# Spreading the next batch's transform steps over the chunks by their VectorE work instead of evenly

## The chip, the cores and the metric

The kernel runs on one core of one Trainium2 chip. TensorE (PE, with its weight loads shown as PEld) multiplies matrices, VectorE (DVE), ScalarE (ACT) and GpSimd (POOL) work element by element, and SyncE (SP), ScalarE and GpSimd have queues on which transfers are issued. The metric is the device time of one execution in microseconds (us): the median of the runs.

## The reference

For 8 batches of 3008 tokens with 256 features, the reference filters along the tokens in the frequency domain and then applies a two-layer network with a gated activation:

```python
X = np.fft.rfft(x, axis=1)                      # x: (8, 3008, 256)
Y = X * (filt_r + 1j * filt_i)[None]
y = np.fft.irfft(Y, n=3008, axis=1).astype(np.float32)
x = y.reshape(8 * 3008, 256)
h = x @ w_in                                    # w_in: (256, 2048)
g = h * (1.0 / (1.0 + np.exp(-1.702 * h)))
return (g @ w_out).astype(np.float32)           # w_out: (2048, 256)
```

## The kernel before

**The network.** The 3008 tokens of a batch are cut into 6 tiles of up to 512 tokens, and the hidden layer of a tile into 16 chunks of 128 features. One pass of the main loop (`for n, (i, fc) in enumerate(turns)`) is one chunk. `first(fc)` of `mlp` multiplies `w_in` with the tile's `y` in six matmuls of 512 columns (L588), because `y` and the weights are held as a high and a low part. ScalarE applies the activation twice, into `gh` (L591) and back into `h` (L592), and VectorE makes the low part `gl = h - gh` (L593). `second(fc)` multiplies `w_out` with `gh` (four matmuls) and `gl` (two), L603. `ahead` issues `first` of the next chunk before `second` of this one. In tile 5 of every even batch (0, 2, 4, 6) the matmuls are 384 columns wide. The first two tiles of batch 0 alternate in the list `turns`, while the generator `conv` still converts weights (up to chunk 23).

**The transform.** The filter of batch b + 1 is made by the generator `fft(b + 1)` while the chunks of batch b run. Each `yield` ends a step, and there are 46 of them:

- 12 steps of stage 1, two for each of the six loads `x_b_c`. ScalarE makes `xh` (L441), GpSimd `xl` (L442), TensorE runs three matmuls (L274 to L276, `s1`), ScalarE copies the sum into `ah` (L446), and VectorE makes `al` (L447). After both halves of a load, four stores on ScalarE's queue put `ah` and `al` into `a_d` in HBM (L452).
- Two empty steps (`for i in range(2): yield`). In front of them `load` brings `a_d` back as `zy` on GpSimd's queue (L461), and `load_f` the filter into `f_buf` on SP's queue.
- 16 steps `forward(i)`: matmuls `s2` (L475 and L476 for i = 0, L478 otherwise), `halves` (L428 on ScalarE, L429 on VectorE) into `c_buf`, the products with the filter into `u_buf` and `c_buf` (L419 to L421 on VectorE), their sum on GpSimd (L422), two casts into `zy` on VectorE (L492) and two subtractions on GpSimd (L493). Each asks for the loads of i + 2.
- 16 steps `backward(i)`, each one behind its forward: matmuls `i2`, `halves` into `b`, and in every second step two stores to `b_d` in HBM on ScalarE's queue (L508).

**The signal.** `signal(b, t, y)` makes the input `y` of tile t: it loads `br` from `b_d` (SP's queue), multiplies (`i1`, L561 and L563), and copies the high part on ScalarE (L569) and the low part on VectorE (L570). In batch 0 `br` comes by transposes `bt` (L543, L547) from SBUF instead.

**What sets the order.** The steps are called in the main loop:

```python
if n % (6 * NFC) == 0:
    lead = 16 if b == 0 else 0
    done, chunk, chunks = 0, 0, 6 * NFC - lead - 8
...
    while chunk <= chunks and done < STEPS * chunk // chunks:
        run(nxt, 1)
        done += 1
```

with `STEPS = 48`, so one step is called about every 1.5 chunks in batch 0 (72 chunks after a lead of 16) and every 1.83 later (88 chunks). The order of the calls is not the final one. A scheduler places the instructions on each engine, in the order of the calls where it can and earlier where it holds an engine for free. It does so as the program is built, by a model of durations; each engine then runs its list strictly in order. Pools limit it too: `ps_f` has four PSUM buffers, and seven `raw` buffers hold `x`, `ah`, `al`, `b` and `br`.

Of the kernel before, what the change touches and what calls it, by code (L numbers as in the profile page):

```python
# [20 lines left out]
P = 128  # L21
Q = 112
NFC = DFF // P
STEPS = 48

LEAST = 2.0**-15
MOST = float(np.uint32(0x47EFFFFF).view(np.float32))
# [125 lines left out]
def tile_kernel(  # L153
# [56 lines left out]
    def load_unit(i):  # L210

        src = (w_out if i % 2 else w_in)[i // 2]
        if i < EARLY:
            w = early[:, i]
            w = w[:, :, :D] if src.dtype == F32 else w.bitcast(I64)
        elif src.dtype == F32:
            w = raw(f"w_{i}").rearrange("p a d -> p (a d)")[:, 0:512].rearrange("p (a d) -> p a d", a=2)
        else:
            w = sb.tile([P, 2, D], I64, tag="raw", name=f"w_{i}", bufs=7)
        load_in(w, src)  # L220
        units[i] = w
# [47 lines left out]
    b_of, stores, done_w = {}, [], [0]  # L269
# [29 lines left out]
    def split_de():  # L299

        pin = tc.keep_in_program_order
        de_f = table["de"].rearrange("p (m c) -> p m c", m=4)
        pin(nc.scalar.copy(t1_sb[:, 0], table["t1"]))
        pin(nc.vector.tensor_tensor(t1_sb[:, 1], table["t1"], t1_sb[:, 0].bitcast(F32), ALU.subtract))
        pin(nc.gpsimd.memset(de_sb.bitcast(F32), 0.0))
        for k in range(2):
            h, o = slice(64 * k, 64 * k + 48), slice(64 - 64 * k, 112 - 64 * k)
            pin(nc.scalar.copy(de_sb[h, k, :, h], de_f[h, :, h]))  # L310
            pin(nc.vector.tensor_tensor(de_sb[h, k, :, o], de_f[h, :, h], de_sb[h, k, :, h].bitcast(F32), ALU.subtract))
            pin(nc.gpsimd.tensor_copy(de_sb[o, k], de_sb[h, k].bitcast(F32)))
# [118 lines left out]
    def fft(b):  # L431
# [22 lines left out]
                    )  # L454

        b_d = dram.tile([48, 64, D], F32, tag="b_d", name=f"b_d{b}")

        def load(i):
            for k in range(2):
                src = a_d[k].rearrange("n (k s) d -> n k s d", k=2)[:, :, 2 * i : 2 * i + 2, :]  # L460
                nc.gpsimd.dma_start(  # L461
                    zy[0][64 * k : 64 * k + 48, i % 2].rearrange("p k s d -> p k (s d)"),
                    src.rearrange("n k s d -> n k (s d)"),
                )
# [51 lines left out]
        for i in range(17):  # L516
# [3 lines left out]
            if i:  # L520
                backward(i - 1)
                yield
        b_of[b] = b_d

    def signal(b, t, y):

# [91 lines left out]
    def store():  # L618

        while stores:  # L620
            nc.sync.dma_start(*stores.pop(0))

    def run(gen, n=None):
        while n is None or n > 0:
            if next(gen, run) is run:
                return False
            n = None if n is None else n - 1
        return True
# [6 lines left out]
    def start(b, t):  # L635
        ys[b, t] = sb.tile([P, 2, 2, 512], F32R, tag="y", name=f"y_{b}_{t}")
        return signal(b, t, ys[b, t])
# [16 lines left out]
    def ahead(i, fc):  # L654
        if i not in chunks_of:
            b, t = tiles[i]
            chunks_of[i] = mlp(b, t, ys.pop((b, t)), 4 if t < 5 or b % 2 else 3, (ps_f, "f") if i == 1 else (ps_o, "o"))
        chunks_of[i][0](fc)

    ahead(*turns[0])  # L660
    for n, (i, fc) in enumerate(turns):
        b, t = tiles[i]
        if n % (6 * NFC) == 0:

            lead = 16 if b == 0 else 0
            done, chunk, chunks = 0, 0, 6 * NFC - lead - 8
            nxt = fft(b + 1) if b + 1 < B else iter(())
        if n == 0:
            run(start(*tiles[1]))
        if n + 1 < len(turns):  # L670
            ahead(*turns[n + 1])
        chunks_of[i][1](fc)
        if fc == 1:
            store()
        if n < 24:
            run(conv, 1)
            if n % 2 and n < 10:
                load_unit(11 + n // 2)
        if n == 9:
            split_de()  # L680
            in_order[0] = False
        if n == 24:
            zy.append(const.tile([P, 4, 2, 2, D], F32R, tag="zy", name="zy"))
            nc.gpsimd.memset(zy[0][32:64].bitcast(F32), 0.0)
        if b or n >= lead:
            chunk += 1
            while chunk <= chunks and done < STEPS * chunk // chunks:
                run(nxt, 1)
                done += 1
        at = () if i == 0 else (10, 11, 13) if i == 1 else (9, 12, 13) if t == 5 else (1, 3, 9)  # L690
        if fc in at and i + 1 < len(tiles):
            if i + 1 not in sigs:
                sigs[i + 1] = start(*tiles[i + 1])
            run(sigs[i + 1], 1)
            if fc == at[-1]:
                run(sigs[i + 1])
# [29 lines left out]
```

## Time and profile before

| | |
|---|---|
| median of 3 runs | 2399.27 us (2398.87 to 2399.83) |
| profiled execution | 2397.69 us, of which its span is 2395.9 us |
| TensorE busy | 2379.6 us (99%) |
| VectorE busy | 1399.9 us (58%) |
| ScalarE busy | 1302.9 us (54%) |
| GpSimd busy | 722.1 us (30%) |
| chain that ended last | TensorE 94% of the span, VectorE 3% |
| loads of `zy` from `a_d`, issue to landing | 3.6 us, 192 KB each |
| stores of `al` to `a_d`, issue to landing | 3.8 us, 256 KB each |

Matmuls are pipelined, so a matmul's recorded span overlaps the next one's: the distance from one start to the next is what it costs. In a row of the timeline stand the start, the duration, engine, line, operation, what is written and read, the shape, the count, and in brackets the idle time before it with what ended that. A wait for several things is put down to the last.

### The profile page before, as it was taken

The page shows a single profiled execution, that of the slowest core. Times are in us where ns is not written, and L with a number is a line of the kernel's source. Part 1 is how long each engine was busy: PE and PEld are TensorE (multiplying, and loading weights), DVE is VectorE, ACT ScalarE, POOL GpSimd, SP SyncE. Part 2 cuts the span into 40 slices and gives each one's busy share as a digit, 9 for nine tenths or more (in the row PEclk, how much of TensorE's full clock was granted, in tenths as well). Part 3 has the DMA queues.
Part 4 walks back from the last instruction along what each step waited for, and adds up shares of the span by engine and source line. Part 5 has one row for each costly group of instructions (what it writes and reads, how often), then busy time and mean ns, then how long its engine had stood idle before and what let it go on. Part 6 is the DMA issues. An engine that isn't in the chain of part 4 may idle for free.

```text
span 2395.9 us, 31327 instructions
## 1 busy us (share of the span) xinstructions
PE 2379.6 (99%) x11102; PEld 1981.7 (83%) x11102; DVE 1399.9 (58%) x2198; ACT 1302.9 (54%) x2426; POOL 722.1 (30%) x675
## 2 busy tenths in 40 slices
PE   9999999999999999999999999999999999999999
PEld 7887888888888889888888888988888888898887
DVE  8967863886357743667436674467734677322222
ACT  6665655655556555555555555555555555444443
POOL 3025532553234422344213442244422344000000
PEclk9999999999999999999999999999999999999999
DMA  9345444643544435443353433534335342300000
GB/s 346 100 137 113 117 128 130 139 119 89 156 95 106 112 102 140 95 101 95 105 136 93 104 97 102 152 92 106 88 104 143 89 106 75 78 7 9 18 9 18
DMA packets 141484, 248.67 MB, mean 104 GB/s; under 512 B 15376, under 2 KB 81040, under 8 KB 141328
## 3 DMA queue, kind: packets, MB, share of 16 engines
q1 hardware_dynamic: 63088, 136.18, 19.6%
q10 hardware_dynamic: 53152, 66.44, 10.3%
q0 software_dynamic: 25088, 44.05, 9.6%
q8 instruction: 88, 1.44, 0.3%
q14 instruction: 68, 0.56, 0.1%
HBM read 152.76 MB, written 93.85 MB: 103 GB/s over the span
## 4 chain that ended last, share of the span: by engine, by line
PE 94%; DVE 3%; DMA 1%; ACT 1%; issue 1%; POOL 0%; SPq 0%; ACTq 0%; POOLq 0%
PE o L603 41%; PE h L588 41%; PE i L561 3%; PE i L478 2%; PE s L478 2%; PE s L274 1%; PE s L276 1%; PE s L275 1%; DVE gl L593 1%; DVE c_buf L429 0%; PE i L391 0%; DVE u_buf L419 0%; DVE u_buf L420 0%; DMA br<-b_d 0%; PE s L381 0%
## 5 line engine op out<-in xcount | busy, mean ns | idle before, releaser
L588 PE MATMUL h<-y,wi 128*128 128x512 f32 (+1 forms) x4608 | 1151.7, 385 | 0.0
L593 DVE TENSOR_TENSOR gl<-h,gh 128x512 fp32r<-128x512 f32 (+1 forms) x768 | 522.3, 680 | 888.3 <-ACT h L592 877.0
L588 PEld LDWEIGHTS h<-y,wi 128*128 128x128 f32 x4608 | 860.6, 188 | 169.7
L591 ACT ACTIVATE gh<-h 128x512 fp32r<-128x512 f32 (+1 forms) x768 | 452.4, 589 | 976.5 <-PE h L588 945.4
L603 PE MATMUL o<-gh,wo 128*128 128x512 f32 (+1 forms) x3072 | 825.7, 388 | 0.5 <-ACT gh L591 0.3
L603 PEld LDWEIGHTS o<-gh,wo 128*128 128x128 f32 x3072 | 570.6, 188 | 114.7 <-ACT gh L591 0.7
L603 PE MATMUL o<-gl,wo 128*128 128x512 f32 (+1 forms) x1536 | 479.3, 389 | 4.5 <-DVE gl L593 4.5
L592 ACT ACTIVATE h<-h 128x512 f32<-128x512 f32 (+1 forms) x768 | 449.2, 585 | 0.0
L493 POOL TENSOR_TENSOR zy<-c_buf,zy 48x512 fp32r<-48x512 f32 x224 | 314.6, 1404 | 85.4 <-DVE zy L492 76.4
L603 PEld LDWEIGHTS o<-gl,wo 128*128 128x128 f32 x1536 | 284.5, 188 | 63.8 <-DVE gl L593 8.8
L422 POOL TENSOR_TENSOR c_buf<-c_buf,u_buf 112x512 f32<-112x512 f32 x127 | 163.9, 1290 | 416.6 <-DVE c_buf L421 416.4
L461 POOL DMA_DIRECT2D zy<-a_d x224 | 128.6, 576 | 351.2 <-PE s L478 187.0
L442 POOL TENSOR_TENSOR xl<-x,xh 128x512 fp32r<-128x512 f32 x84 | 108.3, 1302 | 418.2 <-ACT xh L441 387.2
L429 DVE TENSOR_TENSOR c_buf<-s,c_buf 48x512 f32<-48x512 f32 x224 | 154.2, 689 | 8.8 <-ACT c_buf L428 4.1
L429 DVE TENSOR_TENSOR b<-i,b 48x512 f32<-48x512 f32 x224 | 154.0, 687 | 5.5
L428 ACT COPY c_buf<-s 48x512 f32<-48x512 f32 x224 | 130.1, 581 | 13.5 <-PE s L478 4.1
L428 ACT COPY b<-i 48x512 f32<-48x512 f32 x224 | 130.2, 581 | 11.1 <-PE i L478 5.6
L492 DVE CAST zy<-c_buf 48x512 fp32r<-48x512 f32 x224 | 94.6, 422 | 33.2 <-POOL c_buf L422 28.7
L561 PEld LDWEIGHTS i<-tab,br 128*128 128x128 f32 x736 | 99.3, 191 | 11.0 <-issue 2.2
L561 PE MATMUL i<-tab,br 128*128 128x128 f32 x736 | 100.8, 275 | 1.6 <-DMA br<-b_d 1.5
L420 DVE TENSOR_TENSOR u_buf<-c_buf,f_buf 48x512 f32<-48x512 f32 x112 | 90.8, 811 | 3.6
L419 DVE SCALAR_TENSOR_TENSOR u_buf<-c_buf,f_buf 48x512 f32<-48x512 f32 x112 | 82.2, 734 | 3.6
(95 smaller groups left out, 1124.1 us busy)
## 6 DMA issues: line engine op xcount, KB each, us to landing
f_buf<-fs SPq DMA_DIRECT2D x224, 192.0 KB, 3.2
zy<-a_d POOLq DMA_DIRECT2D x224, 192.0 KB, 3.6
x<-in_x_dram SPq DMA_DIRECT2D x47, 512.0 KB, 5.0
out_dram<-out SPq DMA_DIRECT2D x43, 512.0 KB, 3.3
a_d<-ah ACTq DMA_DIRECT2D x84, 256.0 KB, 3.5
a_d<-al ACTq DMA_DIRECT2D x84, 256.0 KB, 3.8
b_d<-b ACTq DMA_DIRECT2D x112, 192.0 KB, 2.5
br<-b_d SPq DMA_DIRECT2D x84, 256.0 KB, 4.4
```

The costliest lines, as they stand in the source:

```text
L422: eng.tensor_tensor(u1, u1, u2, ALU.add)
L428: nc.scalar.copy(dst[h], ps[k][o])
L429: nc.vector.tensor_tensor(dst[h], ps[k][h], dst[h], ALU.add)
L442: nc.gpsimd.tensor_tensor(xl, src, xh.bitcast(F32), ALU.subtract)
L461: nc.gpsimd.dma_start(zy[0][64 * k : 64 * k + 48, i % 2].rearrange("p k s d -> p k (s d)"), src.rearrange("n k s d -> n k (s d)"),)
L493: nc.gpsimd.tensor_tensor(y[o, k], u1[h], y[h, k].bitcast(F32), ALU.subtract)
L561: nc.tensor.matmul(ps[:, P * i : P * i + P], br[m][:, i], t2_sb, start=True, stop=True)
L588: nc.tensor.matmul(ps[:, :w], wi_sb[half][:, wk, kc, c], y[:, yk, kc, :w], start=n == 0, stop=n == 5)
L591: nc.scalar.activation(gh[:, :w], ps[:, :w], AF.Gelu_apprx_sigmoid)
L592: nc.scalar.activation(ps[:, :w], ps[:, :w], AF.Gelu_apprx_sigmoid)
L593: nc.vector.tensor_tensor(gl[:, :w], ps[:, :w], gh[:, :w].bitcast(F32), ALU.subtract)
L603: nc.tensor.matmul(pos[m][:, :w], wo[:, wk, P * m : P * m + P], gp[gk][:, :w], start=fc == 0 and n == 0, stop=fc == NFC - 1 and n == 2,)
```

## The change

The steps are no longer counted but weighed. A list gives each of the 46 steps a cost: 1.1 for a step of stage 1, 2.6 for each of the two empty ones, 3.2 for a forward, 1.0 for a backward step; the sum is 85.6. In each chunk steps are called as long as the cost already spent is no more than the chunk's share of the sum, over 70 chunks in batch 0 and 86 later. In batch 0 a step of stage 1 is thus called about every 0.9 chunks instead of 1.5, and a forward with its backward every 3.4 chunks instead of 3.0; in later batches it is 1.1 instead of 1.83, and 4.2 instead of 3.67. The last step is called one chunk later than before in every batch.

```diff
-STEPS = 48
+COSTS = [1.1] * 12 + [2.6] * 2 + [3.2] + [3.2, 1.0] * 15 + [1.0]
...
         b_d = dram.tile([48, 64, D], F32, tag="b_d", name=f"b_d{b}")
+        b_of[b] = b_d
...
                 backward(i - 1)
                 yield
-        b_of[b] = b_d
...
             lead = 16 if b == 0 else 0
-            done, chunk, chunks = 0, 0, 6 * NFC - lead - 8
+            spent, chunk, chunks = 0.0, 0, 6 * NFC - lead - 10
+            costs = list(COSTS)
             nxt = fft(b + 1) if b + 1 < B else iter(())
...
             chunk += 1
-            while chunk <= chunks and done < STEPS * chunk // chunks:
+            while costs and spent <= sum(COSTS) * (chunk - 1) / chunks:
                 run(nxt, 1)
-                done += 1
+                spent += costs.pop(0)
```

The line with `b_of` is moved because the generator is no longer run past its last `yield`; it issues nothing. After the change the lines from L457 to L523 stand one lower (L461 becomes L462, L475 becomes L476), and so do those behind L666.

The instructions are the same on every engine; their order is not. Names in the rows below carry batch, tile and chunk (`h_0_2_5`: batch 0, tile 2, chunk 5) or, in the transform, batch, load and half or group (`s1_1_5_1`, `ah_1_5`, `s2_1_0_0`), and a running number at the end.

ScalarE in batch 0, from the last stores of stage 1 of batch 1's transform to the first copy of stage 2, before:

```order
L452 DMA a_d1_1134<-ah_1_5_1613 64x4x256 x2
L452 DMA a_d1_1134<-al_1_5_1614 64x4x256 x2
L569 CAST y_0_3_1655<-i1_0_3_0_1712 128x512
L591 ACTIVATE gh_0_2_5_1726<-h_0_2_5_1719 128x512
L592 ACTIVATE h_0_2_5_1719<-h_0_2_5_1719 128x512
L591 ACTIVATE gh_0_2_6_1744<-h_0_2_6_1737 128x512
L592 ACTIVATE h_0_2_6_1737<-h_0_2_6_1737 128x512
L591 ACTIVATE gh_0_2_7_1762<-h_0_2_7_1755 128x512
L592 ACTIVATE h_0_2_7_1755<-h_0_2_7_1755 128x512
L428 COPY c_buf0_79<-s2_1_0_0_1773 48x512
```

and now:

```order
L452 DMA a_d1_1112<-ah_1_5_1465 64x4x256 x2
L452 DMA a_d1_1112<-al_1_5_1466 64x4x256 x2
L569 CAST y_0_2_1346<-i1_0_2_1_1543 128x512
L591 ACTIVATE gh_0_2_0_1614<-h_0_2_0_1607 128x512
L592 ACTIVATE h_0_2_0_1607<-h_0_2_0_1607 128x512
L591 ACTIVATE gh_0_2_1_1635<-h_0_2_1_1628 128x512
L592 ACTIVATE h_0_2_1_1628<-h_0_2_1_1628 128x512
L591 ACTIVATE gh_0_2_2_1677<-h_0_2_2_1670 128x512
L592 ACTIVATE h_0_2_2_1670<-h_0_2_2_1670 128x512
L428 COPY c_buf0_79<-s2_1_0_0_1648 48x512
```

Stage 1 now ends before chunk 0 of tile 2 and not before chunk 5, and the cast behind the stores is that of tile 2, whose chunks come next. On TensorE, 43 matmuls of 512 columns and the four of an `i1` stood from the last matmul of `s1_1_5_1` (that included) to the first of `s2_1_0_0`; now there are 22 and four.

TensorE in batch 0 around `i1_0_2_1`, the second half of tile 2's signal, before:

```order
L588 MATMUL h_0_2_0_1566<-y_0_2_1300,wi_0_184 128x512 x3
L561 MATMUL i1_0_2_1_1474<-tab_74,br_0_2_1_1472 128x128 x4
L274 MATMUL s1_1_4_0_1532<-xh_1_4_0_1528,t1_sb_75 128x512
L603 MATMUL o_0_1_0_812<-gh_0_1_15_1545,wo_1_940 128x512 x2
L603 MATMUL o_0_1_1_813<-gh_0_1_15_1545,wo_1_940 128x512 x2
L275 MATMUL s1_1_4_0_1532<-xl_1_4_0_1529,t1_sb_75 128x512
L276 MATMUL s1_1_4_0_1532<-xh_1_4_0_1528,t1_sb_75 128x512
L603 MATMUL o_0_1_0_812<-gl_0_1_15_1546,wo_1_940 128x512
L603 MATMUL o_0_1_1_813<-gl_0_1_15_1546,wo_1_940 128x512
L588 MATMUL h_0_2_1_1587<-y_0_2_1300,wi_0_184 128x512 x3
L588 MATMUL h_0_2_0_1566<-y_0_2_1300,wi_0_184 128x512
```

and now:

```order
L275 MATMUL s1_1_5_1_1499<-xl_1_5_1_1496,t1_sb_75 128x512
L276 MATMUL s1_1_5_1_1499<-xh_1_5_1_1495,t1_sb_75 128x512
L561 MATMUL i1_0_2_1_1543<-tab_74,br_0_2_1_1541 128x128 x4
L588 MATMUL h_0_2_0_1607<-y_0_2_1346,wi_0_184 128x512
L588 MATMUL h_0_2_1_1628<-y_0_2_1346,wi_0_184 128x512
L588 MATMUL h_0_2_0_1607<-y_0_2_1346,wi_0_184 128x512 x2
```

The fourth matmul of `h_0_2_0` is the first that reads the half of `y` which `i1_0_2_1` makes. Twelve matmuls stood between the two, and now none.

VectorE in stage 2 of batch 1's transform (batch 0's chunks), from the casts of forward 2 to the product of forward 3, before:

```order
L492 CAST zy_1373<-c_buf2_81 48x512 x2
L420 TENSOR_TENSOR u_buf1_83<-c_buf0_79,f_buf_78 48x512
L419 SCALAR_TENSOR_TENSOR u_buf1_83<-c_buf0_79,f_buf_78 48x512
L593 TENSOR_TENSOR gl_0_3_0_2042<-h_0_3_0_2034,gh_0_3_0_2041 128x512
L610 COPY out_0_2_2052<-o_0_2_1_1600 128x512
L421 TENSOR_TENSOR c_buf0_79<-c_buf0_79,f_buf_78 112x512
```

and now:

```order
L493 CAST zy_1411<-c_buf2_81 48x512 x2
L429 TENSOR_TENSOR c_buf0_79<-s2_1_3_0_1910,c_buf0_79 48x512
L420 TENSOR_TENSOR u_buf1_83<-c_buf0_79,f_buf_78 48x512
L593 TENSOR_TENSOR gl_0_2_9_1872<-h_0_2_9_1864,gh_0_2_9_1871 128x512
L429 TENSOR_TENSOR c_buf0_79<-s2_1_3_1_1911,c_buf0_79 48x512
L419 SCALAR_TENSOR_TENSOR u_buf1_83<-c_buf0_79,f_buf_78 48x512
```

The two products L420 and L419 followed the casts directly and stood ahead of a `gl`; now a `gl` stands between them.

## The prediction

> **What bounds the kernel now.** I read the busy shares first, then the busy time by stretch of 300 us, the chain that ended last, TensorE's waits, and the order of time around each wait.
>
> ```profile
> PE 2379.6 (99%) x11102; PEld 1981.7 (83%) x11102; DVE 1399.9 (58%) x2198; ACT 1302.9 (54%) x2426; POOL 722.1 (30%) x675
> ```
>
> ```profile
> 60.00:360.00 300.00, 293.74 (x1395) 245.14 (x1394) 233.29 (x373) 182.08 (x339) 109.54 (x98) 1.00 0.47 119
> ...
> 660.00:960.00 300.00, 299.93 (x1412) 253.41 (x1411) 178.03 (x278) 165.61 (x312) 101.25 (x96) 1.00 0.44 112
> ```
>
> The columns are the stretch, its length, the busy time of TensorE, its weight loads, VectorE, ScalarE and GpSimd, then granted clock, DMA share and GB/s. TensorE is idle for 6.3 us while batch 0's tokens run and for 0.1 us two batches later. So there is little to win, and it lies in batches 0 and 1.
>
> ```profile
> 605.67 1.36 PE o L603 x6
> 607.03 1.36 PE h L588 x6
> ```
>
> Six matmuls take 1.36 us in the chain, 0.227 each; a chunk is twelve, 2.72 us. The change adds and removes no matmul, so the time moves only with TensorE's waits:
>
> ```profile
> PE o L603 <- DVE gl L593: 4.5, 8, 2.3
> PE i L561 <- DMA br<-b_d: 1.5, 2, 0.9
> PE s L475 <- DMA zy<-a_d: 1.2, 1, 1.2
> ```
>
> (us, times, longest.) A matmul's recorded span, about 0.40, reaches 0.17 past the 0.227 after which the next could start, so each wait is 0.17 more than shown: VectorE's late `gl` cost 4.5 + 8 x 0.17 = 5.8 us, the two waits for `br` 1.8, the one for `zy` 1.4.
>
> **Term 1: the round trip of `a_d` in batch 0, +4.5 us.** Between stage 1 and stage 2 everything goes through HBM:
>
> ```profile
> 174.39 0.39 PE L276 MATMUL s<-xh,t_sb 128*128 128x512 f32 x1
> ...
> 174.82 0.59 ACT L446 CAST ah<-s 128x512 fp32r<-128x512 f32 x1 [0.99 <-PE s L276]
> ...
> 175.44 0.69 DVE L447 TENSOR_TENSOR al<-s,ah 128x512 fp32r<-128x512 f32 x1 [0.88 <-ACT ah L446]
> ...
> 176.73 1.80 ACTq L452 DMA_DIRECT2D a_d<-al  x2
> ...
> 180.32 1.28 POOL L461 DMA_DIRECT2D zy<-a_d  x2 [9.59 <-issue]
> ...
> 186.42 0.35 PE L475 MATMUL s<-zy,de_sb 112*112 112x256 f32 x1 [1.21 <-DMA zy<-a_d]
> ```
>
> ```profile
> 412.56 0.39 PE L276 MATMUL s<-xh,t_sb 128*128 128x512 f32 x1
> ...
> 424.18 0.34 PE L475 MATMUL s<-zy,de_sb 112*112 112x256 f32 x1
> ...
> 666.57 0.39 PE L276 MATMUL s<-xh,t_sb 128*128 128x512 f32 x1
> ...
> 678.81 0.34 PE L475 MATMUL s<-zy,de_sb 112*112 112x256 f32 x1
> ```
>
> From the last matmul of stage 1 to the first of stage 2 takes 12.03 us for batch 1, 11.62 for batch 2, 12.24 for batch 3: copy, subtract, four stores on ScalarE's queue, then GpSimd's loads at +5.9 and their flight. It hardly varies, so TensorE needs that much other work between the two. I count it in the orders, at 0.227 a matmul (0.22 for one of L561's, which is two in the trace, eleven of those in 1.47 us at 597.71 below). Batch 1, before: 43 and four, 10.65 us, wait 1.38. Now: 22 and four, 6.11 us, since stage 1 ends three chunks sooner and stage 2 starts five sooner. The wait becomes 12.03 - 6.11 = 5.9: +4.5. With the other two trips 4.1 or 4.8.
>
> Part of it comes earlier in that stretch. `i1_0_2_1` now has no matmul between itself and the rows of `h_0_2_0` that need its result, and the ScalarE copy which makes that (L569) is queued behind the four stores, which end 4.1 us after L276 by the rows above; about 3.8 us of the 5.9 would be one idle stretch there. It is the same wait, not a second one.
>
> **Term 2: stage 1 itself in batch 0, +0.7.**
>
> ```profile
> 163.26 1.07 PE L588 MATMUL h<-y,wi 128*128 128x512 f32 x4
> 164.60 1.20 PE L603 MATMUL o<-gh,wo 128*128 128x512 f32 x4 [0.27 <-ACT gh L591]
> ```
>
> ```profile
> ACT xh L441 <- issue: 10.6, 10, 2.1
> ```
>
> ```profile
> L442 POOL TENSOR_TENSOR xl<-x,xh 128x512 fp32r<-128x512 f32 x84 | 108.3, 1302 | 418.2 <-ACT xh L441 387.2
> ```
>
> Before, tile 2 starts late (164.60 instead of 163.26 + 4 x 0.227 = 164.17, and about 0.4 more in the next six matmuls): 0.8. That place falls into term 1's wait now. Instead, in the new order `xh` of loads 3 and 5 is queued on ScalarE behind four stores (such waits are the second row), and TensorE has 6.6 and 5.7 us of work between the L276 before and the matmul that needs its `xl`. The stores end at +4.1; the other `xh` ahead of them, this one (0.6 each, as L446 above) and GpSimd's 1.3 make 6.6, and at load 3 a weight cast, taken as 0.6 too, stands between, 7.2: late by 0.6 and 0.9. So 1.5 for 0.8. Bounds: nothing new, -0.8; half a us more each, +1.7. The `x` and `f_buf` loads on SP's queue move with their steps; at the DMA share of 0.47 in the first stretch I cost them at nothing, and without that cover TensorE would wait for `xh` by what is missing of a load.
>
> **Term 3: the same trip in batches 1 to 6, +2.5.** Work between, before and now: batch 2 11.35, 12.03; batch 3 12.01, 11.12; batches 4 and 6 14.22, 10.93; batches 5 and 7 20.18, 12.03. Against trips of 11.62 to 12.24: batch 2 gains 0.2, batch 3 loses 0.3 to 0.9, batches 4 and 6 lose 0.7 to 1.3 each, 5 and 7 up to 0.2. Sum 1.4 to 3.7; I take the middle.
>
> **Term 4: the end of batch 0, -1.05.**
>
> ```profile
> 337.85 0.53 PE h L588 x3
> ```
>
> ```profile
> 336.57 0.40 PE L478 MATMUL i<-zy,de_sb 112*112 112x512 f32 x1
> ...
> 346.18 1.02 PE L561 MATMUL i<-tab,br 128*128 128x128 f32 x7 [0.88 <-DMA br<-b_d]
> ...
> 587.61 0.40 PE L478 MATMUL i<-zy,de_sb 112*112 112x512 f32 x1
> ...
> 597.71 1.47 PE L561 MATMUL i<-tab,br 128*128 128x128 f32 x11 [0.61 <-DMA br<-b_d]
> ```
>
> In tile 5 of an even batch matmuls are narrower, three in 0.53. The trip through `b_d` takes 9.6 us; the work between goes from 8.54 to 11.26, so its wait of 1.05 goes. At the end of batch 1 the work stays 9.31 and the wait 0.8; later batches keep 12.95 and have none.
>
> **Term 5: VectorE's late `gl`, -3.3.**
>
> ```profile
> 216.78 1.66 DVE L420 TENSOR_TENSOR u_buf<-c_buf,f_buf 48x512 f32<-48x512 f32 x1
> 218.47 1.64 DVE L419 SCALAR_TENSOR_TENSOR u_buf<-c_buf,f_buf 48x512 f32<-48x512 f32 x1
> 220.14 0.69 DVE L593 TENSOR_TENSOR gl<-h,gh 128x512 fp32r<-128x512 f32 x1
> ```
>
> ```profile
> 216.38 3.18 POOL L493 TENSOR_TENSOR zy<-c_buf,zy 48x512 fp32r<-48x512 f32 x2 [1.16 <-DVE zy L492]
> ```
>
> ```profile
> 218.21 0.40 PE L478 MATMUL i<-zy,de_sb 112*112 112x512 f32 x1
> 220.89 0.50 PE L603 MATMUL o<-gl,wo 128*128 128x512 f32 x1 [2.28 <-DVE gl L593]
> 221.22 1.09 PE L588 MATMUL h<-y,wi 128*128 128x512 f32 x4
> ```
>
> ```profile
> L420 DVE TENSOR_TENSOR u_buf<-c_buf,f_buf x112: 684/685/1728, 189.0 to 2029.9; 48x512 f32<-48x512 f32 x112
> ```
>
> ```profile
> 973.59 1.57 DVE L420 TENSOR_TENSOR u_buf<-c_buf,f_buf 48x512 f32<-48x512 f32 x1
> ```
>
> The largest wait, 2.45 us, is two products that read `c_buf` and `f_buf`, 0.69 each by the median, stretched by 1.9 while GpSimd runs L493; `gl` is next. Four later batches have one such product (973.59) and lose about 0.4 each. The new order takes the double hit at the first place apart, with a `gl` between. For batches 4 and 6 it puts two products behind the casts, but there `gl` follows h by two chunks' work on TensorE and is due only after it. Batches 5 and 7 lose the place. Single products behind casts stay as frequent (20 places within three rows before, 21 now), so I leave 2.5 of the 5.8. Bounds: all gone, -5.8; nothing gained, 0. Where a stall goes, the next that is late is `a_d`, as above.
>
> **Sum.** 4.5 + 0.7 + 2.5 - 1.05 - 3.3 = +3.35 us on the profiled execution (2395.9 span, 1.8 around it, 2397.69). The median of the runs stands 1.58 higher: 2399.27 + 3.35 = 2402.6. All ends low (4.1, -0.8, 1.4, -1.05, -5.8): -2.2, 2397.1; all high (4.8, 1.7, 3.7, -1.05, 0): +9.2, 2408.4.
>
> **Rivals.**
> (a) Slower: VectorE is blocked as often as before. The products behind casts are 20 and 21; if the late `gl` cost 5.8 again, term 5 is 0 and the time +6.65, 2405.9. It decides from about 1.5 us more lateness than I left. For it: DVE's 233 of 300 us in batch 0 barely changes. Against: stage 2 of batch 0 now ends before tile 5's shorter chunks.
> [...]
> (b) Slower: one idle stretch of 3.8 us halves the clock. What that costs is seen at the start:
>
> ```profile
> L293 PE MATMUL idle<-zero 128*128 128x512 f32 x8 | 3.6, 629 | 1.1 <-DVE zero L342 1.1
> ```
>
> Eight matmuls in 3.6 us instead of 8 x 0.227 + 0.17 = 2.0: 1.6 once, 2404.2. It decides only on top of the forecast. Against: after 2.45 us of idleness at 218 four matmuls took 1.09 with the last one's span of 0.40, still 0.23 each.
> [...]
> (c) Same: all late `gl` vanish (-5.8) and terms 1 to 4 stand: +0.85, 2400.1.
> (d) Same: the scheduler cancels the new spacing. It does in part: the last steps of batches 4 to 7 stand where they stood. Were it so throughout, 2399.3; the 6.11 us speak against it.
> (e) Faster: the trip of `a_d` shrinks with its stores drawn together, and term 1 turns into the gain of 1.4, term 3 into 0.5: -1.4 + 0.7 - 0.5 - 1.05 - 3.3 = -5.55, 2393.7. Against: three trips within 0.6 us of each other.
>
> **Chances.** What a measurement tells from no change is 0.2%, 4.8 us: 2394.5 to 2404.1. Forecast 0.50 (0.45 of it within, 0.05 above), (a) 0.20, (b) 0.05, (c) 0.12, (d) 0.07, (e) 0.06. Faster 0.06, same 0.45 + 0.12 + 0.07 = 0.64, slower 0.05 + 0.20 + 0.05 = 0.30. The range leaves out (e) and the outermost ends: 2398 to 2407.
>
> **What would show it.** Term 1: around 165 us, L561 of `i1_0_2_1` followed by an idle TensorE of 3 to 4 us ended by ScalarE's `y`, and L476 (after's line) still waiting for `zy`; TensorE's idle in batch 0 grows beyond 6.3. Term 3: waits for `zy` about 1 us long near 960 and 1550. Term 4: no wait for `br` near 346. Term 5: TensorE's wait for `gl` at 2 to 3 us in all. I am wrong if the trip in batch 0 is much under 11.6 us, or if `gl` waits grow past 6.

## The result and the profile after

The change makes the kernel slower: 2418.14 us median of five runs (2417.24 to 2420.78) against 2398.88 for five runs of the kernel before beside them, a ratio of 1.0082 (95% interval 1.0071 to 1.0093). The forecast of 2402.6, with 2398 to 2407 around it, was 15.5 us too low. The profiled execution took 2419.0 us, its span 2417.2, 21.3 more than before.

TensorE's waits in the profile after (what waited, for whom; us in all, times, longest):

```profile
PE s L476 <- DMA zy<-a_d: 7.7, 6, 3.3
PE o L603 <- DVE gl L593: 7.0, 9, 2.1
PE h L588 <- ACT y L569: 3.5, 1, 3.5
PE i L561 <- DMA br<-b_d: 1.6, 2, 0.9
PE s L274 <- ACT xh L441: 1.4, 1, 1.4
```

`zy` was 1.2 us in one wait and is 7.7 in six; `y` is new; `gl` went from 4.5 to 7.0. The busy time of stretches of 300 us (columns as before: TensorE first, near the end the granted clock) shows that batch 0 is no longer the only place:

```profile
60.00:360.00 300.00, 289.81 (x1349) 238.95 (x1349) 232.48 (x370) 179.70 (x334) 109.52 (x99) 0.99 0.46 118
...
1260.00:1560.00 300.00, 296.69 (x1375) 249.46 (x1374) 173.86 (x274) 162.59 (x304) 99.00 (x92) 0.99 0.42 105
```

The clock reads 0.99 there. Short stretches at both places show two times at half rate:

```profile
165.00:171.88 6.88, 3.10 (x18) 1.99 (x16) 1.98 (x3) 2.51 (x5) 1.28 (x1) 0.94 0.81 245
171.88:177.60 5.72, 5.47 (x12) 3.93 (x13) 2.08 (x3) 2.29 (x5) 2.39 (x4) 0.50 0.99 204
...
1267.10:1273.30 6.20, 5.92 (x16) 4.88 (x17) 2.87 (x5) 2.25 (x4) 1.11 (x2) 0.50 0.31 65
1273.30:1279.50 6.20, 6.20 (x31) 5.15 (x31) 3.86 (x8) 2.67 (x5) 2.87 (x3) 0.98 0.25 66
```

16 matmuls in 6.2 us, then 31. A busy TensorE is not a fast one: in the second row it counts 5.47 of 5.72 us as busy and does half the work.

To say where the time went I took, in both traces, every matmul's time to the start of the next, less the median for its kind (line, tiles and shape), and grouped what exceeds it by what the next one waited for. The waits are those above plus 0.17 each:

| TensorE's excess, us | before | after |
|---|---|---|
| wait for `zy` | 1.4 | 8.7 |
| wait for `y` in batch 0 | 0 | 3.7 |
| half clock, beyond the waits | 0 | 5.8 |
| late `gl` | 5.8 | 8.9 |
| `xh`, `xl` | 0.5 | 2.4 |
| `br` | 1.8 | 1.9 |
| `gh`, and the copy `out` once | 0.9 | 0 |
| all else | 21.2 | 21.2 |
| sum | 31.6 | 52.6 |

By the 15th chunk of batch 0's last tile the execution is 9.5 us behind. From the same chunk of batch 2 to that of batch 3 another 8.8 come (the waits that end at 973 and 1267 us), the remaining 3.0 in all other batches together.

### The profile page after: what moved, and what is told of

Its sections match the earlier page's. It is cut to its first block, busy times and chain, and to the rows that moved or that the text cites. A ratio compares the mean times of both kernels' runs of the same rounds, so it can differ in the third digit from the quotient of the medians.

```text
span 2417.2 us, 31365 instructions
## 1 busy us (share of the span) xinstructions
PE 2387.8 (99%) x11102; PEld 1985.4 (82%) x11102; DVE 1409.0 (58%) x2198; ACT 1303.9 (54%) x2426; POOL 723.4 (30%) x675
## 4 chain that ended last, share of the span: by engine, by line
PE 88%; DVE 5%; issue 3%; DMA 3%; POOL 1%; ACT 1%; ACTq 0%; SPq 0%; POOLq 0%; DVEq 0%
PE o L603 39%; PE h L588 39%; PE i L561 3%; PE i L479 2%; PE s L479 2%; DMA zy<-a_d 1%; DVE gl L593 1%; PE s L274 1%; DVE c_buf L429 1%; PE s L275 1%; DVE u_buf L419 1%; DVE u_buf L420 1%; PE s L276 1%; DMA br<-b_d 0%; DMA x<-in_x_dram 0%
## 5 line engine op out<-in xcount | busy, mean ns | idle before, releaser
L588 PE MATMUL h<-y,wi 128*128 128x512 f32 (+1 forms) x4608 | 1154.5, 386 | 3.5 <-ACT y L569 3.5
L593 DVE TENSOR_TENSOR gl<-h,gh 128x512 fp32r<-128x512 f32 (+1 forms) x768 | 522.1, 680 | 899.9 <-ACT h L592 894.4
L588 PEld LDWEIGHTS h<-y,wi 128*128 128x128 f32 x4608 | 862.2, 188 | 173.6 <-ACT y L569 3.7
L603 PE MATMUL o<-gh,wo 128*128 128x512 f32 (+1 forms) x3072 | 827.1, 389 | 0.0
L603 PEld LDWEIGHTS o<-gh,wo 128*128 128x128 f32 x3072 | 571.5, 189 | 116.1 <-ACT gh L591 1.9
L603 PE MATMUL o<-gl,wo 128*128 128x512 f32 (+1 forms) x1536 | 480.0, 389 | 7.1 <-DVE gl L593 7.0
L603 PEld LDWEIGHTS o<-gl,wo 128*128 128x128 f32 x1536 | 285.0, 189 | 67.1 <-DVE gl L593 12.4
L462 POOL DMA_DIRECT2D zy<-a_d x224 | 128.8, 577 | 343.1 <-PE s L479 137.3
L429 DVE TENSOR_TENSOR c_buf<-s,c_buf 48x512 f32<-48x512 f32 x224 | 154.2, 688 | 13.1 <-ACT c_buf L428 8.4
L561 PEld LDWEIGHTS i<-tab,br 128*128 128x128 f32 x736 | 98.6, 191 | 11.1 <-issue 1.3
L561 PE MATMUL i<-tab,br 128*128 128x128 f32 x736 | 100.5, 275 | 1.7 <-DMA br<-b_d 1.6
L420 DVE TENSOR_TENSOR u_buf<-c_buf,f_buf 48x512 f32<-48x512 f32 x112 | 95.2, 850 | 3.6
L419 DVE SCALAR_TENSOR_TENSOR u_buf<-c_buf,f_buf 48x512 f32<-48x512 f32 x112 | 82.4, 736 | 3.6
```

The lines of the kernel that those rows point to most:

```text
L420: nc.vector.tensor_tensor(u2[64:Q], xs[0:48], f_i[0:48], ALU.mult)
L429: nc.vector.tensor_tensor(dst[h], ps[k][h], dst[h], ALU.add)
L462: nc.gpsimd.dma_start(zy[0][64 * k : 64 * k + 48, i % 2].rearrange("p k s d -> p k (s d)"), src.rearrange("n k s d -> n k (s d)"),)
L561: nc.tensor.matmul(ps[:, P * i : P * i + P], br[m][:, i], t2_sb, start=True, stop=True)
L588: nc.tensor.matmul(ps[:, :w], wi_sb[half][:, wk, kc, c], y[:, yk, kc, :w], start=n == 0, stop=n == 5)
L593: nc.vector.tensor_tensor(gl[:, :w], ps[:, :w], gh[:, :w].bitcast(F32), ALU.subtract)
```

## The experiments

### Which part, and where

**Batch 0 even, the rest as changed** (e3), and its complement (e13); the edit is shown shortened:

```diff
-            while costs and spent <= ...:
+            while b == 0 and chunk <= chunks and done < 48 * chunk // chunks:   # 72 chunks
+                run(nxt, 1); done += 1
+            while b and costs and spent <= ...:                                  # e13: b and b == 0 exchanged
```

> The changed kernel, but in batch 0 (the transform of batch 1) the steps are spread evenly and over 72 chunks as before; batches 1 to 6 keep the new costs. Theory (the loss is the dense stage 1 and the short way from stage 1 to stage 2: of 21.3 us in the profiled executions 9.5 have come by the end of batch 0): 9.5 less, 2408.6, and the time near 1264 with its half clock stays as it is. Rival (the loss in batch 0 is the one that moves the later batches too, since each batch's stage 1 starts where the one before left the engines): back to 2399 to 2402.

> The changed kernel's costs in batch 0 alone; batches 1 to 6 have 48 even steps and two chunks more, as before: the complement of the run with batch 0 even, which took 7.3 us off the changed kernel. Work between the stages 5.4 us for batch 1 and as before for batches 3 to 7. Theory (the losses of batch 0 and of the later batches are separate and add up): 2399.5 + 9.5 by the trace of the changed kernel, 2409; no wait for zy above 1.5 us after batch 2, no half clock after 200 us. Rival (batch 0 moves what comes later): 2404 or below, or 2414 or above.

Measured: 2410.83 (ratio 1.0045, 1.0031 to 1.0059) and 2411.92 (1.0055, 1.0041 to 1.0069). So the later batches alone cost 11.4 us, batch 0 alone 12.3; together 23.7, where the whole change costs 18.6 by the same baseline. Each direction held, the sizes were 2 to 3 us off, and the two do not simply add; why not stays open.

**Two chunks fewer alone** (e1: the kernel before, `- 8` made `- 10`) and **the costs alone** (e14: the changed kernel, `- 10` made `- 8`):

> The kernel before with its 48 even steps over two chunks fewer (86, in batch 0 70): the second half of the change alone. Work between the stages by the order as before but for batch 2 (10.3 instead of 11.0 us). Theory (the two chunks cost nothing but that trip): 0.7 us more, 2400.2. Rival (the denser steps make VectorE late all along): 2405 or above, by waits for gl.

> The changed kernel with its new costs over the old number of chunks (88, in batch 0 72): the first half of the change alone. Work between the stages by the order: 8.2 us for batch 1, 12.7 for batches 2 and 3, 10.7, 10.9, 10.7, 10.9 for batches 4 to 7 (changed kernel 5.4, 11.8, 10.9, 10.7, 11.8, 10.7, 11.8). Theory A (the trips of a_d decide): 2.7 us less waiting in batch 0 and one half clock less there, 2 less in batches 2 and 3, 2 more in 5 and 7: 2418 - 4 = 2414. Theory B (the two chunks carry 13 whatever the steps): 2405. Theory C (the halves do not add, either alone costs nearly the whole): 2416 or more.

Measured: 2412.63 (1.0055, 1.0042 to 1.0069) and 2414.65 (1.0065, 1.0053 to 1.0078). The first was a plain miss: 13.0 instead of 0.7. The second took the time of theory A, but not by its terms. In its trace the half clock near 172 us is gone, as A has it, but another stands near 135; the waits for `zy` in batches 2 and 3 fell from 1.1 us to 0.7 and not by 2; and late `gl`, which A left alone, fell from 7.0 us to 4.3. That the number fits is in part luck. Either half alone costs most of the whole. Of the e1 trace's 16.7 us, 8.0 are there by the end of batch 0, with the same 2.45 us for `gl` at 218, more of them later, and three times at half clock:

```profile
PE o L603 <- DVE gl L593: 7.0, 9, 2.3
PE s L475 <- DMA zy<-a_d: 2.4, 2, 1.3
PE o L603 <- ACT gh L591: 1.3, 3, 0.6
```

In its later batches 1 to 1.6 us each are spread over many matmuls, a few ns apiece, with no wait to name; that part stays open.

**Stage 1 at the mean cost** (e2: `COSTS = [2.1] * 14 + [3.2] + [3.2, 1.0] * 15 + [1.0]`), and **forward and backward at the mean cost** (e11: `[1.1] * 12 + [2.6] * 2 + [2.1] * 32`):

> The changed kernel with stage 1 and the two empty steps at the mean cost of 2.1 each instead of 1.1 and 2.6; forward and backward keep 3.2 and 1.0, and the two chunks fewer stay. Work on TensorE between the last matmul of stage 1 and the first of stage 2, by the order: 10.0 us for batch 1, 10.3, 11.3, 11.0, 11.3, 11.0, 11.3 for batches 2 to 7. Theory (every trip of a_d that is longer than the work is paid in full): 2.0 + 1.9 + 0.9 + 1.3 + 1.0 + 1.3 + 1.0 us of waits for zy where before had 3, no half clock, so some 6 slower than before: 2405, up to 2409 if the late loads near 1260 stay and the wait there is long. Rival A (only the dense stage 1 costs, forward and backward by their work are free): 2399. Rival B (it is the spacing of forward and backward, by late gl): 2410 to 2418 with gl waits of 7 us or more.

> The changed kernel with the costs of forward and backward made equal (2.1 each; stage 1 and the empty steps keep 1.1 and 2.6): the complement of the run with stage 1 at the mean. Work between the stages: 5.4, 10.0, 10.9, 10.7, 11.8, 10.7, 11.8. Theory (the trips are what costs, and the dense stage 1 sets them in batch 0): about as slow as the changed kernel, 2418 to 2420. Rival (the spacing of forward and backward carries half of the loss): 2409.

Measured: 2415.05 (1.0065, 1.0053 to 1.0078) and 2424.61 (1.0107, 1.0092 to 1.0122). In e2 the trace stands only 0.3 us behind before at the end of batch 0; everything is lost later, to `zy`, with three times at half clock and less late `gl` than before (3.3 against 4.5):

```profile
PE s L476 <- DMA zy<-a_d: 9.7, 5, 4.3
PE o L603 <- DVE gl L593: 3.3, 6, 1.6
```

That is the theory in kind, but for the half clock, which it left out; it is 6 to 10 us above it in size, and not rival B. e11 is 6.5 us slower than the whole change, beyond what either side expected: late `gl` is no worse there (5.6), but `br` is late seven times (4.4 us) and the clock is halved four times.

### Covering the trip

**A longer pause** (e5: 6.0 for each empty step instead of 2.6):

> The changed kernel with a cost of 6.0 instead of 2.6 for each of the two empty steps, and nothing kept in order: work between the stages 10.7 us instead of 5.4 for batch 1; 11.3, 10.4, 10.8, 11.3, 10.8, 11.3 for batches 2 to 7 (11.8, 10.9, 10.7, 11.8, 10.7, 11.8 in the changed kernel). Theory (in batch 0 the short way between the stages and its half clock cost 3.7 + 0.4 + 2.9 us): a wait of 1.5 stays there, so 5.5 less, the other trips 1.5 more: 2414. Rival (the wait was only moved: stage 2 in fewer chunks makes gl later by as much): 2418 or more, with gl waits of 10 us.

Measured: 2412.95 (1.0057, 1.0044 to 1.0070), 5.2 us less than the changed kernel and near the theory's time, but by other amounts. Of the difference between the two traces 3.3 us arise in batch 0, where the theory had 5.5, and 3.5 later, where it had 1.5 more: all waits for `zy` grew to 10.8 us from 7.7, but late `gl` fell to 3.3 from 7.0. So covering the trip helps in batch 0; that the sum fits is luck.

**Stage 2 held at its place** (e8, in batches 2 to 7; e9 in batch 1 too, with the pause; e10 the same in the kernel before):

```diff
-                    nc.tensor.matmul(ps[k][:Q, 0], de_sb[:, k, m + 1], ...)
+                    first = nc.tensor.matmul(ps[k][:Q, 0], de_sb[:, k, m + 1], ...)
+                    if m == k == 0 and b > 1:          # e9, e10: b > 0
+                        tc.keep_in_program_order(first)
```

> The changed kernel with the first matmul of stage 2 kept in program order in batches 2 to 7, so that it comes where the costs put it and not as soon as the scheduler thinks that its data are there: TensorE's work between stage 1 and stage 2 goes from 11 to 12 us to 29 for batch 2 and 62 to 67 for batches 3 to 7; batch 1 keeps its 5.4 (by the order). Theory (in the later batches the loss is the uncovered trip of a_d and the half clock behind the longest wait): the waits for zy of 0.7, 0.8, 1.8, 3.5, 1.3 and 0.6 us go, 8.7 in all, and the clock's 2.8: 11.5 less, 2406.6. Rival (the packed stage 2 behind makes VectorE and the trip of b_d late): waits for gl and br grow past 12 us and the time stays above 2412.

> As the run before, in batch 1 too, and the two empty steps between the stages cost 6.0 each instead of 2.6: work between stage 1 and stage 2 is 17.5 us for batch 1, 40 for batch 2, 64 to 78 after that (by the order). Theory (uncovered trips and the clock are nearly the whole loss): beside the 11.5 us of the run before, the idle stretch for y, the wait for zy and the half clock in batch 0 go, 3.7 + 0.4 + 2.8 = 6.9: 2399.7, the time of the kernel before. What stays is the stall of 2.1 us at 131.5 from the dense stage 1 among the weight conversions. Rival (stage 2 in fewer chunks makes gl late): above 2405, with gl waits of 10 us and more.

> The kernel before (48 even steps) with the first matmul of stage 2 kept in program order in batches 1 to 7: work between the stages 10.4 us for batch 1, 39 for batch 2, 67 to 75 after that (by the order). Theory (the trip of a_d costs what is not covered): its waits for zy in batches 2 and 3, 0.3 to 0.9 us each, go, the one of batch 1 shrinks by 0.4: about 1.5 less, 2397.9. Rival (before, the early stage 2 left more room for VectorE at the end of a batch): slower, 2402 or above, by waits for gl in tile 5.

Measured: 2420.45 (1.0087, 1.0073 to 1.0100), 2431.25 (1.0131, 1.0115 to 1.0147) and 2406.76 (1.0031, 1.0020 to 1.0043). All three theories fell and the rivals' times stood (e10's late `gl`, 9.7 us in 21 waits, came all along the batches and not in tile 5). The waits for `zy` did go wherever stage 2 was held, but for 0.7 us in batch 1 of e10 (the 0.9 us below is batch 1's, which e8 leaves as it is); what came for them, in e8 and then in e9 (there L605 is the network's L603, L595 is L593 and L563 is L561):

```profile
PE o L605 <- DVE gl L595: 12.8, 18, 2.0
...
PE s L476 <- DMA zy<-a_d: 0.9, 1, 0.9
```

```profile
PE o L605 <- DVE gl L595: 26.7, 28, 2.0
PE i L563 <- DMA br<-b_d: 6.1, 7, 1.1
```

One such place in e9, one of the recurring ones:

```profile
1181.42 3.22 POOL L496 TENSOR_TENSOR zy<-c_buf,zy 48x512 fp32r<-48x512 f32 x2 [1.92 <-DVE zy L495]
...
1181.83 1.67 DVE L420 TENSOR_TENSOR u_buf<-c_buf,f_buf 48x512 f32<-48x512 f32 x1
...
1183.53 1.67 DVE L419 SCALAR_TENSOR_TENSOR u_buf<-c_buf,f_buf 48x512 f32<-48x512 f32 x1
...
1185.22 0.69 DVE L595 TENSOR_TENSOR gl<-h,gh 128x512 fp32r<-128x512 f32 x1
```

It is the double hit of 218 us, now once in each of the batches 1 to 6 (a wait of 1.6 us each), beside smaller ones. A stage 2 that starts late is squeezed, and VectorE pays for it; one that starts early leaves `a_d` uncovered. The order before lies between the two.

### What the half clock costs

**14 matmuls of zeros in the idle stretch of batch 0** (e4), behind `i1_0_2_1`:

```diff
+            if (b, t, m) == (0, 2, 1):
+                warm(bt[-1].rearrange("p a b -> p (a b)"), 14)
```

`warm(ps, n)` is `n` matmuls of the tile `zero`; `bt[-1]` is the PSUM buffer of the transposes in front.

> The changed kernel with 14 matmuls of zeros put into TensorE's idle stretch of 3.7 us behind i1_0_2_1 in batch 0, and nothing else moved; the like stretch of 3.5 us near 1264 us is left as it is, as a control. Theory of the clock (an idle stretch of this length halves the clock for 6.8 us, and the work in those 6.8 us then takes 2.8 us more than at full rate): the granted clock shows no 0.5 near 172 us, h_2_0 and o_2_0 take 0.227 a matmul there, the 0.5 near 1267 stays, and the time falls by 2.8 to 2415.3. Rival (the time is lost in the waits alone, the slow matmuls behind them make up for it later in another wait, for example that for zy): the time stays at 2418.1 within 0.5.

Measured: 2417.36 (1.0075, 1.0062 to 1.0088), 0.8 less than the changed kernel. The half clock near 172 us is gone, as expected, and the time is not. First the changed kernel, then e4 (lines up to ten higher: L598 is L588, L577 L569, L483 L476):

```profile
172.13 2.93 PE L588 MATMUL h<-y,wi 128*128 128x512 f32 x6 [3.50 <-ACT y L569]
```

```profile
168.56 3.43 PE L301 MATMUL bt<-zero 128*128 128x512 f32 x14
...
172.72 1.94 PE L598 MATMUL h<-y,wi 128*128 128x512 f32 x6 [0.73 <-ACT y L577]
...
180.57 0.34 PE L483 MATMUL s<-zy,de_sb 112*112 112x256 f32 x1 [1.47 <-DMA zy<-a_d]
```

The six matmuls of h take 1.94 us instead of 2.93, and TensorE then waits 1.47 for `zy`, for which it did not wait in the changed kernel. The rival had it: slow matmuls fill the time of the trip, and fast ones leave TensorE idle for the rest of it. Stage 2 starts 12.7 us behind stage 1 in the changed kernel and 13.1 in e4, whose trace is 0.4 us behind the other's at the end of batch 0. What e4 is faster by comes later, and 1.3 us of it at the place left as a control: there the half clock lasted 3.41 us instead of 6.83.

Where nothing covers it, the half clock is paid. Two executions have the same order and the same stall of 2.28 us at 218, the kernel before and e3; only the second fell to half clock behind it:

```profile
220.89 0.50 PE L603 MATMUL o<-gl,wo 128*128 128x512 f32 x1 [2.28 <-DVE gl L593]
221.22 1.54 PE L588 MATMUL h<-y,wi 128*128 128x512 f32 x6
```

```profile
221.06 0.80 PE L603 MATMUL o<-gl,wo 128*128 128x512 f32 x1 [2.28 <-DVE gl L593]
221.65 2.69 PE L588 MATMUL h<-y,wi 128*128 128x512 f32 x6
```

Up to there they are 0.17 us apart, 10 us later 1.62: 1.45 us for one stretch of 3.41 us at half rate.

### The late loads near 1260

In the changed kernel's profile, at the longest of the waits for `zy`:

```profile
1251.90 0.39 PE L276 MATMUL s<-xh,t_sb 128*128 128x512 f32 x1
...
1252.43 0.59 ACT L592 ACTIVATE h<-h 128x512 f32<-128x512 f32 x1
1252.94 0.59 ACT L446 CAST ah<-s 128x512 fp32r<-128x512 f32 x1
...
1261.35 2.25 POOL L462 DMA_DIRECT2D zy<-a_d  x4 [13.30 <-issue]
...
1267.38 0.53 PE L476 MATMUL s<-zy,de_sb 112*112 112x256 f32 x1 [3.31 <-DMA zy<-a_d]
```

The loads leave 9.45 us behind the last matmul of stage 1 instead of some 6.5. Before, the same loads are as late, but with 20 us of work to hide them:

```profile
1241.00 0.39 PE L276 MATMUL s<-xh,t_sb 128*128 128x512 f32 x1
...
1250.12 2.25 POOL L461 DMA_DIRECT2D zy<-a_d  x4 [16.89 <-issue]
...
1261.17 0.28 PE L475 MATMUL s<-zy,de_sb 112*112 112x256 f32 x1
```

**32 memsets on GpSimd ahead of all** (e6: `nc.gpsimd.memset(pad, 0.0)`, `pad` a tile of its own of 128 x 8), then **8 small DMAs on its queue** (e7: `nc.gpsimd.dma_start(pad[:, 8 * i : 8 * i + 8], tabs[:, 0:8])`), and these with the old number of chunks (e18):

> The changed kernel with 32 small memsets on GpSimd ahead of everything, where GpSimd is idle; the order of every other instruction stays. Theory (the zy loads near 1261 us leave 3.4 us after their last wait because GpSimd's next block of instructions arrives just there: a packet of the instruction queue starts at 1257.6 and the load is about the 644th of GpSimd's instructions in the trace, 5 x 128 + 4): the block's border moves elsewhere, the loads leave at +6 to +6.5 us behind the last matmul of stage 1 as in the other batches, the wait near 1264 falls from 3.5 to about 0.5 and no half clock follows, 3.0 + 2.8 less: 2412.3. A border that falls into another such place would give part of it back. Rival (the loads are late because a store lands late, or because the DMA rings are busy): nothing changes, 2418.1.

> The changed kernel with 8 small DMAs (128 x 32 bytes each) on GpSimd's queue ahead of everything; the order of all other instructions stays. In six traces so far, before and after alike, the 129th DMA that GpSimd issues leaves 3.43 us after its last semaphore; in the changed kernel that is the first zy load of batch 5. The run with 32 more memsets on GpSimd moved its place among the instructions (676th instead of 644th) and changed nothing, so it is not the count of instructions. Theory (it is the count of GpSimd's DMAs): the stall moves to a load of stage 2 in batch 3, which is issued two steps ahead of its use; the loads near 1260 us leave at +6 to +6.5, the wait there falls from 3.5 to about 0.5, no half clock follows, and the time falls by 3.0 + 2.8, to 2412.3. Rival (it belongs to this place, say the first use of this buffer or the traffic there): 2418, wait of 3.5 as before.

> The new costs over the old number of chunks, and 8 small DMAs on GpSimd's queue ahead of everything, which move its 129th DMA off the trip of batch 5. Theory: against the same without the 8 DMAs the wait of some 4.5 us near 1260 falls to about 1.5 and its half clock goes: 4.5 less, 2409.5 if that stands at 2414. Rival (the loss of later batches lies elsewhere): no less than 2 of it.

Measured: e6 2424.81 (1.0105, 1.0092 to 1.0119), with the late loads where they were: the theory of the instructions fell. (Why it is 6.7 us slower is open; its trace has 2.1 us more of waits for `zy` and one more time at half clock.) e7 2415.01 (1.0065, 1.0052 to 1.0078), 3.1 less than the changed kernel, and the place looks as foreseen:

```profile
1256.71 0.39 PE L276 MATMUL s<-xh,t_sb 128*128 128x512 f32 x1
...
1263.21 1.15 POOL L462 DMA_DIRECT2D zy<-a_d  x2 [10.35 <-issue]
...
1269.13 0.35 PE L476 MATMUL s<-zy,de_sb 112*112 112x256 f32 x1 [0.25 <-DMA zy<-a_d]
```

6.5 us instead of 9.45, a wait of 0.25 instead of 3.31, and the granted clock behind it is 1.00:

```profile
1269.10:1275.30 6.20, 6.17 (x33) 5.39 (x34) 4.73 (x7) 3.12 (x7) 1.91 (x3) 1.00 0.31 67
```

So the eight DMAs take the stall away from this load. That it goes with the count of DMAs is not shown: by the theory it had to move to the new 129th, a load of `zy` at 1104 us, and that one left 0.50 us behind its last semaphore, as did the 129th of e18; no load of the two traces left more than 1 us behind. From the end of batch 2 to the end of batch 3 e7's trace loses 1.7 us against before, the changed kernel's 7.6: the 5.8 foreseen are there (5.9). That only 3.1 show in the median (the runs go from 2412.3 to 2418.5) fits its trace, which was 14.8 us behind instead of 9.5 by the end of batch 0, with half clock at other places, near 135 and 347 us. e18 took 2411.16 (1.0052, 1.0039 to 1.0064), 3.5 less than e14 and not the 4.5 expected.

### A version that beats both

If spacing by VectorE's work is good for `gl` and bad only where it uncovers `a_d`, it belongs into batch 0, whose trip the mean cost for stage 1 keeps covered. e16 has e2's costs in batch 0 over the old 72 chunks, and even steps over 88 in all others; e17 has 70 in batch 0.

> The kernel before in all batches but batch 0; there stage 1 and the empty steps have the mean cost and forward and backward the new 3.2 and 1.0, over the old 72 chunks. Work between the stages 11.3 us for batch 1 instead of 10.0, the rest as before. Theory (spacing by VectorE's work is good for gl where the trip stays covered): the stall of 2.45 us at 218 goes, the wait for zy in batch 0 shrinks by 1.3, and no half clock can follow: 2 to 3 us faster than before, 2396.5 to 2397.5. Rival (gl is late elsewhere instead): 2399 to 2401.

> As the run before, with two chunks fewer in batch 0 alone (70). In the run with these costs in all batches the trace stood 0.3 us behind that of the kernel before at the end of batch 0. Theory (in batch 0 the spacing by VectorE's work makes up for the two chunks, and the later batches, even as before, lose nothing): 2399.8. Rival (two chunks fewer cost in batch 0 whatever the spacing, 8 with even steps): 2405 to 2408.

Measured: e16 2394.92 (0.9983, 0.9974 to 0.9992), faster than before, by 3.8 us where 2 to 3 were expected; e17 2398.06 (0.9996, 0.9987 to 1.0005), the same. e16's waits:

```profile
PE i L561 <- DMA br<-b_d: 2.1, 2, 1.2
PE o L603 <- DVE gl L593: 1.7, 6, 0.5
```

Late `gl` falls from 4.5 us to 1.7, longest 0.5 instead of 2.3. So in batch 0 the spacing of forward and backward does what the change sets out to do; in all batches, with a short stage 1 and two chunks fewer, it comes with more than it brings.

## Why the prediction was wrong, step by step

In TensorE's excess, after less before, by the terms of the sum:

| term | forecast | measured |
|---|---|---|
| 1, trip of `a_d` in batch 0 | +4.5 | +5.2 |
| 2, stage 1 in batch 0 | +0.7 | +2.3 |
| 3, trips of batches 2 to 7 | +2.5 | +11.6 |
| 4, `b_d` at the end of batch 0 | -1.05 | +0.1 |
| 5, late `gl` in stage 2 | -3.3 | +0.7 |
| not foreseen: `xh` at 641 us | 0 | +1.5 |
| not foreseen: the copy `out` at 273 us | 0 | -0.4 |
| sum | +3.35 | +21.0 (span +21.3) |

**Term 1** was right in mechanism and place: the idle stretch of 3.5 us ended by `y` is there, its cause the copy behind four stores. The trip took 12.7 us instead of 12.0 with 6.1 of work, so 6.6 of delay: 3.7 idle, the rest in matmuls at half clock. The forecast expected a further wait for `zy` there; the slow matmuls filled it, and e4 shows the exchange.

**Term 2** missed a wait of 2.1 us (2.3 in the excess) for `gl` at 132 us; of the 1.5 that it foresaw for `xh` and `xl` 0.85 came. A denser stage 1 puts GpSimd's `xl` beside VectorE's weight conversions, which still run there (L254 takes 0.69 us by its median):

```profile
131.75 1.35 POOL L442 TENSOR_TENSOR xl<-x,xh 128x512 fp32r<-128x512 f32 x1 [2.46 <-ACT xh L441]
...
132.00 1.65 DVE L254 TENSOR_TENSOR w_tu<-w_tu 128x512 f32<-128x512 f32 x1
```

I counted ScalarE's queue there and not VectorE's.

**Term 3 is the step that failed most.** The work beside the trips was counted right; their length was not. The forecast took one length, 11.6 to 12.2 us, from the three trips whose end showed. The order moved other work into them, and they took 11.9 to 12.8 us and in batch 5 15.5: in five of the six `ah` waits behind a pair of activations (the rows at 1252) and starts 0.8 to 1.05 us behind its matmul, not 0.43. So batches 3, 4 and 6 waited where the forecast put it, for 0.8, 1.8 and 1.3 us, and batches 2, 5 and 7, which were to lose 0.2 at most, for 0.7, 3.5 and 0.6. The wait of batch 4:

```profile
973.50 0.34 PE L476 MATMUL s<-zy,de_sb 112*112 112x256 f32 x1 [1.67 <-DMA zy<-a_d]
```

Batch 5's late loads stood in the trace before, under 20 us of other work, and I did not look at trips that nothing waited for. Then comes the clock: 2.9 us behind the longest wait, which nothing hides. Of the 9.1 us missed here, 2.9 are the late loads, 2.9 the clock and 3.3 the longer trips; e7 confirms the first two, the third is read from the rows alone.

**Term 4** fell because the trip of `b_d` went from 9.6 to 12.4 us: its last store waits on ScalarE 3.3 us behind its matmul instead of 2.0, and on SP's queue a store of `out` now stands between the two loads of `br`. I had counted the work beside the trip as moved and the trip as fixed.

**Term 5** had the sign wrong. The stall at 218 us went, as forecast, and others came: five of 0.65 to 1.2 us in batch 0, two of 0.9 later. The mean of L420 grew from 811 to 850 ns, so VectorE was blocked more and not less; rival (a) named this, at 5.8 us where 6.5 came. At five of the seven places a product took 1.58 to 1.67 us beside GpSimd's subtract, just ahead of `gl`; at 268 and 323 us none is stretched, and two products of 0.69 us stand in line ahead of `gl`. In e9's rows above, L420 and L419 took 1.67 us each beside that subtract too. How often an order brings the two together only the trace of that order showed.

**Rival (b)** came true twice, at a chance of 0.05, and at 2.9 us each time where it had 1.6. I argued that a stall of 2.45 us had left the clock alone. It had, by its phase: the like stall halved the clock in e3, where the granted clock from 220.5 to 223.9 us reads 0.53 and in the kernel before 1.00. The last section has the idle times that half clock followed in these traces.

## What to carry to other kernels

A trip through memory that nothing waits for has no length in the list of waits; before taking its cover away, read its own rows in every place, since the longest may be the best hidden one, as batch 5's was here (before, its loads left 9.1 us behind stage 1, and TensorE, with 20 us of other work, waited for none of them). When steps are respaced, recount both sides of each trip, the work beside it and what now stands in its queues, and expect a gain on one wait (`gl`, 7.0 to 3.3 us in e5) to be paid in another (`zy`, 7.7 to 10.8): try it where the trip stays covered first, as e16 does. And no half of a table change can be taken as free: two chunks fewer alone cost 13 us.

## What the hardware showed

**The half clock came on a grid of 3.413 us.** In the changed kernel's trace its two stretches inside the work begin 48.00 and 369.00 windows of that length behind the clock's first record and last two windows each. Over the 18 traces of this case, up to the last 12 us of each, 29 windows of that grid at full clock showed at least 1.81 us without a matmul, and each was followed by half clock; none with 1.60 us or less was, and of 13 in between 2 were. (In the last 12 us one window with 1.88 us was not.) So in these traces about half a window idle was enough (1.81 us and more of 3.413), and a stall of 2.1 us halved the clock or didn't by where it fell: the one at 132 us did in e6, e7, e9, e11, e14 and e18 and did not in the changed kernel, e4, e5, e8 and e13. It lasted one window or two. By the 1.45 us above, such a stall could set two runs of one kernel that far apart.

**The 129th DMA that GpSimd issues left 3.43 us after the wait in front of it had ended**, in all sixteen traces without the eight extra DMAs (3.43 or 3.44), wherever it stood among the instructions. With them, in e7 and e18, no load left more than 1 us behind, neither batch 5's nor the new 129th. So the eight DMAs end the stall, but whether their number, their size or something else does it is open. An instruction packet of 8 KB, which gave the theory of e6, does not explain it: in e8, e9, e10 and e14 none starts within 5 us of the end of that wait, and in e7 one starts there, at 1262.6 us, and batch 5's load leaves in time.
